# A fused gate, state-space and linear-attention kernel: the flag transpose becomes the last TensorE instruction, SP issues in emission order, and the hand-written order list is replaced

## The chip, the cores and the metric

The kernel runs on one core of a Trainium2 chip. The core has five engines with a queue of instructions each: TensorE (PE, matrix products), VectorE (DVE), ScalarE (ACT), GpSimd (POOL) and SyncE (SP, which computes nothing here and issues DMA transfers). They meet at semaphores. Each engine takes its instructions in the order of its own queue.

The metric is the device time of one execution in microseconds, here the median of nine.

## The reference

One input sequence x of 2048 rows and 512 columns goes through two branches, and a gate mixes them row by row.

```python
g = sigmoid((x * gate_w).sum(-1, keepdims=True))
# A: a diagonal complex state-space recurrence
Lam_bar = exp(dt * Lam);  Bu = einsum("bld,pd->blp", x, B_bar)
for t in range(L): h = Lam_bar * h + Bu[:, t];  hs.append(h)
a = 2 * einsum("blp,dp->bld", hs, Cmat).real + x * Dskip
# B: linear attention, 32 heads of 16
q, k, v = split(x @ wqkv)
phi_q = cat(softmax(q @ w_phi), softmax(-(q @ w_phi)));  phi_k likewise
kv = einsum("bhsf,bhsd->bhfd", phi_k, v);  z = phi_k.sum(s)
b = (phi_q @ kv / (phi_q @ z + 1e-6)) @ wo
return g * a + (1 - g) * b
```

## The kernel before

The 2048 rows are taken as 512 groups of four (`F = 4`), so row 4r + f belongs to phase f, and each phase is cut into four tiles of 128. The state space is handled in four scans (`scan_unit`, j = 0 to 3). For each, PE projects x with B (`g_unit`, line 676) and folds the phases (line 681), ACT or DVE copy the result out of PSUM into the tile `Gs` or, for the last phase, into a buffer `c` (lines 377 and 379). SP rearranges that buffer with four DMAs (`xd`, line 690, called the swap below), DVE rotates it and runs the recurrence (lines 714 to 732), and eight DMAs put the states into `Zs` (`zd`, line 744). `fill_unit` (lines 756 to 764) then derives the other three phases on DVE. The output matrix is scaled into an `ET` buffer (lines 599 and 604) and stored into `CT` with eight DMAs (`ctd`, line 611).

For the attention, `v_unit` (449) and `k_unit` (788, 812, 819) build the values, the key features and their sums; `q_unit` (876) and `smalls` build the query features and the scales. `mix` (line 972) then makes one output tile of 128 rows: four products with the key-value blocks (985), a copy by ACT (988) and scaling and adding by DVE (992, 994) into `o2`; a DMA transpose of `o2` to `oT` on SP (1009); the state-space product with `CT` (1001) and the skip term (1005) on PE; the product with `Wo` into the same PSUM (1017, function `pb`); the scaling by the gate on ACT or DVE (1022 or 1024, function `of`) and the output DMA (1028, `od`), on SP's or ACT's queue. The very last tile is made in two halves of 256 columns.

The fast path is valid only for inputs within limits. DVE collects them (`fl1`, 1047 to 1050), PE transposes the column of verdicts (1052), DVE reduces it to one integer (`fl2`, 1055 and 1056), and every engine loads that integer (`values_load`, 1062) and branches (line 162) past the code of a general path that stands behind.

What runs in which order is decided by a planner, `_Plan`. Every step is a task with an estimated cost for each engine that may run it, and the tuple `ORDER` gives the sequence in which tasks are placed and emitted; an entry is twice the task's number, plus one where the second engine listed takes it. The planner's times only choose buffers; `ORDER` fixes the sequence. `deps` and `follow` of a task enter those times, no semaphore comes from them. The set `ENGINES` (line 211) names the engines whose instructions stay in the order of emission. SP is not in it: its instructions are reordered by the language's own scheduler. Every engine's instructions wait at semaphores for the data and the buffers that they use. SP's queue does not pass over an instruction that waits.

Of the kernel before, what the change touches and what calls it, by code (L numbers as in the profile page):

```python
# [18 lines left out]
P = 128  # L19
# [103 lines left out]
def kernel(  # L123
# [58 lines left out]
    564, 422, 482, 400, 552, 484, 464, 466, 108, 486, 220, 222, 600, 554, 488, 110, 402, 566, 364, 410, 574, 556,  # L182
    412, 414, 224, 374, 216, 492, 468, 186, 626, 494, 112, 490, 594, 576, 416, 188, 496, 578, 558, 232, 376, 114,
    116, 218, 596, 234, 118, 580, 424, 604, 120, 498, 426, 598, 246, 602, 500, 428, 236, 692, 238, 606, 694, 584,
    226, 630, 248, 696, 430, 228, 122, 586, 632, 230, 628, 686, 588, 608, 640, 124, 642, 250, 718, 688, 458, 240,
    610, 724, 590, 560, 432, 126, 434, 252, 690, 592, 242, 722, 244, 612, 634, 726, 636, 644, 366, 652, 638, 370,
    128, 720, 728, 698, 582, 700, 654, 656, 198, 666, 372, 254, 646, 702, 616, 256, 668, 730, 368, 618, 648, 650,
    670, 704, 786, 200, 732, 436, 258, 734, 614, 278, 708, 658, 280, 660, 774, 710, 834, 620, 790, 792, 788, 662,
    736, 828, 672, 202, 816, 778, 712, 622, 838, 776, 836, 822, 740, 742, 796, 204, 624, 260, 664, 818, 714, 744,
    674, 716, 746, 780, 794, 748, 262, 826, 676, 832, 756, 752, 750, 824, 810, 130, 754, 820, 798, 784, 782, 812,  # L190
    814, 804, 1204, 846, 850, 852, 830, 802, 678, 738, 806, 848, 808, 854, 264, 1222, 840, 1216, 800, 856, 1210,
    948, 1226, 680, 858, 842, 862, 864, 950, 946, 844, 682, 866, 944, 868, 902, 1224, 1212, 1036, 870, 952, 860,
    976, 884, 1214, 954, 978, 996, 1002, 998, 878, 956, 984, 1076, 970, 1004, 1078, 980, 1080, 1048, 960, 972,
    958, 1074, 684, 1022, 974, 1050, 1062, 1006, 1000, 1024, 1054, 1056, 982, 1010, 1052, 1008, 1206, 872, 1028,
    962, 988, 1058, 964, 1060, 1218, 1038, 966, 1030, 968, 1014, 986, 1082, 1026, 1064, 874, 1084, 880, 1208,
# [6 lines left out]
    1198, 1282, 1148, 1177, 1350, 918, 1294, 1266, 1346, 1316, 1250, 1310, 1286, 1272, 1348, 1318, 1296, 920, 938,  # L202
    1284, 1252, 1288, 1200, 1290, 1364, 1366, 1352, 1416, 1292, 1358, 926, 1150, 1410, 1268, 922, 1270, 1324,
    1368, 1360, 1418, 932, 928, 1298, 1124, 1412, 1320, 1384, 1274, 924, 1420, 1202, 1414, 1390, 1322, 1362, 930,
    1276, 1422, 934, 1326, 936, 1386, 1278, 1370, 1300, 1428, 1436, 1372, 1328, 940, 942, 1424, 1392, 1442, 1376,
    1438, 1302, 1394, 1444, 1398, 1374, 1388, 1426, 1354, 1331, 1396, 1430, 1046, 1400, 1432, 706, 1440, 1446,
    1448, 1450, 1242, 1402, 1088, 772, 1305, 1435, 1378, 1357, 1380, 1468, 1404, 1454, 1452, 1407, 1409, 1456,
    1470, 1472, 1458, 1462, 1465, 1382, 1466, 1461)
KR = 0
GR = 0  # L210
ENGINES = {mybir.EngineType.PE, mybir.EngineType.DVE, mybir.EngineType.Activation, mybir.EngineType.Pool}


def _pe(n, cols):
    return {"PE": n * max(30.0, cols / 2.4 + 3.0)}


def _dve(*elems):
    return {"DVE": sum(e / 0.96 + 70.0 for e in elems)}


def _act(*elems):
    return {"ACT": sum(e / 1.2 + 100.0 for e in elems)}
# [3 lines left out]
def _fast_path(ctx, tc, A_x, A_Lambda_re, A_Lambda_im, A_B_re, A_B_im, A_C_re, A_C_im, A_log_dt, A_Dskip,  # L227
               B_wqkv, B_w_phi, B_wo, gate_w, out):
    nc = tc.nc
# [15 lines left out]
    def ctile(shape, dt, name):  # L245
        return const.tile(shape, dt, name=name)
# [9 lines left out]
    ident = ctile([P, P], BF16, "ident")  # L256
# [28 lines left out]
    fb = ctile([P, 2], BF16, "fb")  # L285
# [17 lines left out]

    ctx.enter_context(tc.manual_schedule(engines=ENGINES))

# [42 lines left out]
    pl = _Plan({"DVE": 2.4e3, "ACT": 5.6e3, "PE": 1.1e3, "SP": 27.0e3})  # L348
# [12 lines left out]
    def f32v(b):  # L361
        return b.t[:]

    def bfv(b):
        return b.t[:].bitcast(BF16)[:, 0:512]
# [18 lines left out]
    d_wv0, d_wv, d_b, d_wk, d_wq, d_wo = (pl.at(t) for t in (4.8, 5.6, 17.0, 22.7, 24.8, 27.0))  # L384
    d_vec, d_wc = pl.at(9.5), pl.at(20.5)

    def tcols(f, a):
        return slice(f * NCH + a * P, f * NCH + (a + 1) * P)
# [38 lines left out]
    for a in range(4):  # L427
# [5 lines left out]
        t = pl.add({"PE": 460.0} if a < 2 else _pe(4, 128), tr, deps=[d_x[a // 2]], follow=[t_warm], bufs=[b, early[0]])  # L433
# [145 lines left out]
    for jj in range(2):  # L579
        parts = []  # L580
        for tt in range(4 * jj, 4 * jj + 4):
# [3 lines left out]
                           deps=parts, rank=6 - jj))  # L585
# [10 lines left out]
    for j in range(PT):  # L596
        done = []
        for ri in range(2):
            done.append(pl.add(_act(640), lambda e, j=j, ri=ri: nc.scalar.mul(out=tC[:, ri, :], in_=cb.t[:, 1 - ri, j, :], mul=nb2i[:, j:j + 1]),
                               deps=[tp6, t_cl] + tc_b[-2:], bufs=[cb], rank=2))  # L600
# [15 lines left out]
    for jj in range(2):  # L616
# [10 lines left out]
        def tb3(e):  # L627
# [4 lines left out]
                    deps=[x2, t_trig], bufs=[early[2]], rank=5)  # L632
# [283 lines left out]
    def lb(k0, n, shape=None, dt=BF16):  # L916
        def make(k):
            if not late:
                late.append(wk.tile([P, NTI * H * (Dh + 1)], BF16, tag="vx", name="late", bufs=1))
            v = late[0][:, k0 + k * n:k0 + (k + 1) * n]  # L920
            v = v if dt is BF16 else v.bitcast(dt)
            return v if shape is None else v.rearrange("p (a b) -> p a b", a=shape)
        return make
# [2 lines left out]
    pl.pool("al", 2, lb(12 * D, 4 * 2 * H, 4))  # L926
    pl.pool("ot", 4, lb(13 * D, D))
    t_al, als, t_qm = {}, {}, []

    def smalls(f, rank=0.0):  # L930
        pl.unit("smalls")
# [40 lines left out]
    def mix(f, a, rank=0.0):  # L972
        pl.unit("mix")
        ti = f * 4 + a
        cs = slice(a * P, (a + 1) * P)
        last = (f, a) == (FO[3], 3)
        pys = [pl.buf(*A3) for _ in range(2 if last else 1)]
        w = D // len(pys)
        pn = [pl.buf(*A2), pl.buf(*A2)]
        o2 = pl.buf("o2")  # L980
        tm = []
        for sgn in range(2):
            def nm(e, sgn=sgn):
                for g in range(HG):
                    MM(out=f32v(pn[sgn])[:, g * P:(g + 1) * P], lhsT=ets[f].t[:, sgn, g, cs], rhs=KVbd[:, sgn, g, :], start=True, stop=True)  # L985
            t = pl.add(_pe(4, 128), nm, deps=t_kvx + [t_al[f]], bufs=[pn[sgn], ets[f], o2], rank=rank + 2)

            tn = pl.add(_act(512), lambda e, sgn=sgn: nc.scalar.copy(out=o2.t[:, sgn], in_=f32v(pn[sgn])), deps=[t], bufs=[pn[sgn], o2], rank=rank + 2)  # L988

            def sc(e, sgn=sgn):  # L990
                v = o2.t[:, sgn].rearrange("p (g d h) -> p g d h", g=HG, d=Dh)
                VT(out=v, in0=v, in1=als[f].t[:, a, sgn * H:(sgn + 1) * H].rearrange("p (g h) -> p g h", g=HG).unsqueeze(2).to_broadcast([P, HG, Dh, 8]), op=ALU.mult)  # L992
            tm.append(pl.add(_dve(256), sc, deps=[tn, t_al[f]], bufs=[o2, als[f]], rank=rank + 2))
        x = pl.add(_dve(256), lambda e: VT(out=o2.t[:, 0], in0=o2.t[:, 0], in1=o2.t[:, 1], op=ALU.add), deps=tm, bufs=[o2], rank=rank + 2)
        yh = []
        for hh in range(2):
            def ym(e, hh=hh):
                for tt in range(4 * hh, 4 * hh + 4):
                    st = Zs[:, 0, tt, ZP + a * P:ZP + (a + 1) * P] if f == 3 else Gs[:, tt, f, cs]
                    for n, py in enumerate(pys):  # L1000
                        MM(out=f32v(py)[:, 0:w], lhsT=st, rhs=CT[:, tt // 2 + 4 * (tt % 2), n * w:n * w + w], start=(tt == 0), stop=False)  # L1001
                if hh == 1:
                    for kt in range(KT):
                        c0 = kt * P % w
                        MM(out=f32v(pys[kt * P // w])[:, c0:c0 + P], lhsT=xT[:, kt, tcols(f, a)], rhs=Dd[:, kt, :], start=False, stop=False)
            c = _pe(4, 512)["PE"] + (hh * _pe(4, 128)["PE"])
            yh.append(pl.add({"PE": c}, ym, deps=[(t_z[j] if f == 3 else t_h[j, f]) for j in (2 * hh, 2 * hh + 1)] + [t_ct] + t_dd, follow=yh[-1:], bufs=pys, rank=rank))
        oT = pl.buf("oT")
        t = pl.add({"SP": 1200.0}, lambda e: nc.sync.dma_start_transpose(out=oT.t, in_=o2.t[:, 0]), deps=[x], bufs=[oT, o2], rank=rank + 3, xl={"SP": 700.0})

        ot = pl.buf("ot")
        for n, py in enumerate(pys):
            hs = slice(n * w, n * w + w)

            def pb(e, py=py, hs=hs):
                for g in range(HG):
                    MM(out=f32v(py)[:, 0:w], lhsT=oT.t[:, g, :], rhs=Wo[:, g, hs], start=False, stop=(g == HG - 1))  # L1017
            tb = pl.add(_pe(4, w), pb, deps=[t, d_wo], follow=yh[-1:], bufs=[py, oT], rank=rank + 3)

            def of(e, py=py, hs=hs):  # L1020
                if e == "ACT":
                    nc.scalar.mul(out=ot.t[:, hs], in_=f32v(py)[:, 0:w], mul=Gg[:, ti:ti + 1])  # L1022
                else:
                    VS(out=ot.t[:, hs], in0=f32v(py)[:, 0:w], scalar1=Gg[:, ti:ti + 1], scalar2=None, op0=ALU.mult)
            to = pl.add({"ACT": w / 1.2 + 200.0, "DVE": w / 0.96 + 135.0}, of, deps=[tb, t_gg], bufs=[py, ot], rank=rank + 3)

            def od(e, hs=hs):
                (nc.scalar if e == "ACT" else nc.sync).dma_start(out=o4[a, :, f, hs], in_=ot.t[:, hs])
            pl.add({"SP": 600.0, "ACT": 600.0}, od, deps=[to], bufs=[ot], rank=rank + 3, xl={"ACT": 1800.0 + 700.0 * (not last), "SP": 400.0 + 700.0 * (not last)})
# [14 lines left out]
    bf_ = pl.buf(*A2)  # L1044
# [4 lines left out]
        nc.vector.tensor_reduce(out=fl[:, 3:4], in_=fl[:, 0:3], axis=AX.X, op=ALU.max)  # L1049
        VS(out=fb[:, 0:1], in0=fl[:, 3:4], scalar1=GATE_LIMIT, scalar2=None, op0=ALU.is_le)  # L1050
    x = pl.add({"DVE": 600.0}, fl1, deps=t_qm + [t_fk, t_tn], rank=20)
    x = pl.add({"PE": 60.0}, lambda e: nc.tensor.transpose(bfv(bf_)[0:1, 0:P], fb[:, 0:1], ident[:]), deps=[x], bufs=[bf_], rank=20)

    def fl2(e):
        nc.vector.tensor_reduce(out=ff[:, 0:1], in_=bfv(bf_)[0:1, 0:P], axis=AX.X, op=ALU.min)
        VS(out=flag_i[:], in0=ff[:, 0:1], scalar1=-1.0, scalar2=1.0, op0=ALU.mult, op1=ALU.add)
    pl.add({"DVE": 400.0}, fl2, deps=[x], bufs=[bf_], rank=20, xl={"DVE": 2500.0})

    pl.run()
    tc.mark_branch_hint_location("general", engines=(mybir.EngineType.PE, mybir.EngineType.DVE, mybir.EngineType.Activation))  # L1060
# [622 lines left out]
```

## Time and profile before

| | |
|---|---|
| nine runs, median | 153.94 us |
| nine runs, lowest and highest | 153.58 and 155.66 us |
| profiled execution, its time | 154.16 us |
| profiled execution, its span | 152.4 us |
| ACT busy | 108.4 us (71%) |
| DMA moved | 14.96 MB, mean 98 GB/s |
| DMA transposes of `late` (line 1009), issue to landing, min / median / max | 2.4 / 2.5 / 3.9 us |

The span runs from the first to the last recorded instruction; the device time has some start and end around it. Rows give the start or the busy time in us, the line of the kernel, the engine, the operation and the tiles as output <- input; "SPq" and "ACTq" are an engine's queue, in which DMAs are issued. A number in brackets is idle time of that engine just ahead, and what ended it. Pool buffers taken late in the kernel are all called `late`, PSUM buffers `pp`.

### The profile page before, as it was taken

The numbers are of one execution on the slowest core, as the hardware profiler recorded it, in microseconds if no ns is written. First come the engines' busy times: TensorE is split into PE (matmuls) and PEld (weight loads), VectorE is DVE, ScalarE is ACT, GpSimd is POOL, SyncE is SP. The second block draws the span as 40 slices with busy tenths as digits, with TensorE's granted clock in tenths as the row PEclk, the third lists the DMA queues.
The fourth block names the chain that finished last, engine by engine and source line by source line (L and its number), as shares of the span: only waits on it lengthen the run. The fifth ranks groups of instructions, "written<-read, shape, count | busy, mean of one in ns | idle before, by whom it ended". The sixth has DMA issues, their size and how long they took to land.

```text
span 152.4 us, 3149 instructions
## 1 busy us (share of the span) xinstructions
PE 142.0 (93%) x1105; PEld 82.6 (54%) x1124; DVE 131.0 (86%) x373; ACT 108.4 (71%) x218; POOL 5.3 (3%) x16
## 2 busy tenths in 40 slices
PE   6699999999999999999999999999999999999930
PEld 1344667455656665465446556566556455555720
DVE  2349999899999999998999999899999999998120
ACT  3149978999789798987999999759754845373110
POOL 8500000000000000000000000000000000000000
PEclk9999999999999999999999999999999999999995
DMA  3999999900320333223530313232661185035430
GB/s 103 304 208 234 163 237 221 195 6 0 69 69 0 80 94 103 52 68 96 128 79 29 96 47 99 52 69 38 74 170 35 34 108 137 0 77 121 123 107 3
DMA packets 37260, 14.96 MB, mean 98 GB/s; under 512 B 29432, under 2 KB 37240, under 8 KB 37240
## 3 DMA queue, kind: packets, MB, share of 16 engines
q1 hardware_dynamic: 35488, 13.33, 40.7%
q10 hardware_dynamic: 1592, 1.38, 3.1%
q8 instruction: 10, 0.16, 0.5%
q14 instruction: 10, 0.08, 0.2%
q0 software_dynamic: 160, 0.01, 0.1%
HBM read 1.60 MB, written 2.10 MB: 24 GB/s over the span
## 4 chain that ended last, share of the span: by engine, by line
PE 41%; DVE 35%; DMA 9%; ACT 4%; SPq 4%; issue 2%; DVEq 0%; ACTq 0%
PE pp L1001 9%; PE pp L676 8%; PE pp L449 7%; PE pp L788 6%; PE pp L1017 5%; DMA Zs<-c 5%; DVE c L724 5%; DMA xn<-in_A_x_dram 3%; DVE c L760 3%; DVE E L812 3%; DVE late L992 3%; DVE st L805 2%; DVE ET L604 2%; SPq L744 2%; DVE c L757 2%
## 5 line engine op out<-in xcount | busy, mean ns | idle before, releaser
L676 PE MATMUL pp<-xT,BT 128*128 128x512 bf16 x122 | 30.6, 381 | 0.2
L1001 PE MATMUL pp<-CT,Gs 128*128 128x512 bf16 (+1 forms) x101 | 23.5, 362 | 0.4
L676 PEld LDWEIGHTS <-BT 128*128 128x128 bf16 x128 | 17.8, 145 | 8.5
L988 ACT CAST late<-pp 128x512 bf16<-128x512 f32 x32 | 17.8, 591 | 6.1 <-PE pp L985 5.0
L240 ACT ACTIVATE E<-pp 128x512 bf16<-128x512 f32 x32 | 17.4, 614 | 2.3 <-PE pp L819 1.7
L240 ACT ACTIVATE ET<-pp 128x512 bf16<-128x512 f32 x32 | 17.3, 602 | 0.4 <-PE pp L876 0.3
L1022 ACT ACTIVATE late<-pp,Gg 128x512 bf16<-128x512 f32 (+1 forms) x15 | 10.1, 679 | 10.0 <-PE pp L1017 7.1
L1017 PE MATMUL pp<-Wo,late 128*128 128x512 bf16 (+1 forms) x65 | 15.6, 366 | 0.2
L788 PE MATMUL pp<-Wk,xT 128*128 128x512 bf16 x64 | 15.8, 379 | 0.0
L449 PE MATMUL pp<-Wv,xT 128*128 128x512 bf16 x63 | 15.2, 379 | 0.3 <-DVE xT L379 0.3
L876 PE MATMUL pp<-xT,Wq 128*128 128x512 bf16 x61 | 14.5, 379 | 0.2
L1001 PEld LDWEIGHTS <-Gs 128*128 128x128 bf16 x104 | 9.5, 98 | 8.3 <-DVE Gs L764 1.1
L992 DVE TENSOR_TENSOR late<-late 128x512 bf16<-128x512 bf16 x32 | 12.8, 426 | 0.0
L377 ACT CAST Gs<-pp 128x512 bf16<-128x512 f32 x18 | 10.3, 598 | 3.4 <-PE pp L676 2.0
L985 PE MATMUL pp<-KVbd,ET 128*128 128x128 bf16 x128 | 11.3, 219 | 0.0
L985 PEld LDWEIGHTS <-ET 128*128 128x128 bf16 x128 | 8.7, 98 | 3.7
L377 ACT CAST vx<-pp 128x512 bf16<-128x512 f32 x16 | 8.9, 594 | 2.1 <-PE pp L449 2.1
L788 PEld LDWEIGHTS <-xT 128*128 128x128 bf16 x64 | 6.2, 98 | 7.2
L812 DVE TENSOR_TENSOR E<-E,rc 128x2048 bf16<-128x2048 bf16 x8 | 9.7, 1220 | 0.4 <-ACT rc L240 0.4
L876 PEld LDWEIGHTS <-Wq 128*128 128x128 bf16 x64 | 6.0, 98 | 6.6
L449 PEld LDWEIGHTS <-xT 128*128 128x128 bf16 x64 | 5.9, 98 | 6.8 <-DVE xT L379 0.5
L724 DVE TENSOR_TENSOR_SCAN c<-sp,c 128x512 bf16<-128x512 f32 x8 | 9.3, 1210 | 0.0
(171 smaller groups left out, 242.6 us busy)
## 6 DMA issues: line engine op xcount, KB each, us to landing
Zs<-c SPq DMA_DIRECT2D x32, 64.0 KB, 2.1
c<-c SPq DMA_DIRECT2D x16, 64.0 KB, 2.0
CT<-ET SPq DMA_DIRECT2D x8, 128.0 KB, 3.0
out_dram<-late ACTq DMA_DIRECT2D x8, 128.0 KB, 1.9
out_dram<-late SPq DMA_DIRECT2D x7, 128.0 KB, 1.9
xn<-in_A_x_dram SPq DMA_DIRECT2D x2, 256.0 KB, 4.3
Wo<-in_B_wo_dram SPq DMA_DIRECT2D x4, 128.0 KB, 3.1
Wv<-in_B_wqkv_dram ACTq DMA_DIRECT2D x1, 256.0 KB, 4.2
```

The lines of the kernel that those rows point to most:

```text
L240: return nc.scalar.activation(**kw)
L377: nc.scalar.copy(out=o, in_=view(b))
L449: MM(out=f32v(b), lhsT=xT[:, kt, tcols(f, a)], rhs=Wv[:, kt, :], start=(kt == 0), stop=(kt == KT - 1))
L676: MM(out=f32v(b), lhsT=BT[:, kt].rearrange("p r (q t) -> p (r q) t", t=NT)[:, :, j + 4 * h], rhs=xT[:, kt, f * NCH:(f + 1) * NCH], start=( ...
L724: nc.vector.tensor_tensor_scan(out=bw_.t[:, ri], data0=rb, data1=b1.t[:, ri], initial=0.0, op0=ALU.mult, op1=ALU.add)
L788: MM(out=f32v(b), lhsT=xT[:, kt, tcols(f, a)], rhs=Wk2[:, kt, :], start=(kt == 0), stop=(kt == KT - 1))
L876: MM(out=f32v(b), lhsT=Wq2[:, kt, g * P:(g + 1) * P], rhs=xT[:, kt, f * NCH:(f + 1) * NCH], start=(kt == 0), stop=(kt == KT - 1))
L985: MM(out=f32v(pn[sgn])[:, g * P:(g + 1) * P], lhsT=ets[f].t[:, sgn, g, cs], rhs=KVbd[:, sgn, g, :], start=True, stop=True)
L988: tn = pl.add(_act(512), lambda e, sgn=sgn: nc.scalar.copy(out=o2.t[:, sgn], in_=f32v(pn[sgn])), deps=[t], bufs=[pn[sgn], o2], rank=rank + 2)
L992: VT(out=v, in0=v, in1=als[f].t[:, a, sgn * H:(sgn + 1) * H].rearrange("p (g h) -> p g h", g=HG).unsqueeze(2).to_broadcast([P, HG, Dh, 8]) ...
L1001: MM(out=f32v(py)[:, 0:w], lhsT=st, rhs=CT[:, tt // 2 + 4 * (tt % 2), n * w:n * w + w], start=(tt == 0), stop=False)
L1017: MM(out=f32v(py)[:, 0:w], lhsT=oT.t[:, g, :], rhs=Wo[:, g, hs], start=False, stop=(g == HG - 1))
```

## The change

The task of the flag's transpose gets a `follow` on the last `pb`, the estimate of the flag's way is changed, SP joins the set of engines that keep emission order, and `ORDER` is a new list. As written, the list moves few tasks: the flag's transpose and reduction stand behind the last product with `Wo` (the tail `1470, 1472` moves behind `1462`), the scaling of the second half of the last tile goes from DVE to ACT (`1465` becomes `1464`), one ACT copy of `Gs` (`628`) comes ahead of an ACT scaling and a small activation, one DVE reduction into `smax` (`706`) comes six instructions earlier, and a task of ACT (`844`) and one of SP (`1428`) move against tasks of other engines. On PE nothing else moves.

Because SP now follows the list, its queue changes more. The four swaps of scan 1 stand together, the first of them waiting for the later of two tiles; scan 2's four swaps stand ahead of scan 1's stores to `Zs`; the eight stores to `CT`, spread over the scans before, stand together behind the swaps of scan 3. Behind the `Zs` stores came, in order, with T a transpose and O an output: TTTTO TTTO TO TTO TO TTO TTTO, the flag's load, O. Now it is TTTTTTTO TTTO TTOOO TTO TTO O, the flag's load, with the sixth and seventh T in the other order.

```diff
-    226, 630, 248, 696, 430, 228, 122, 586, 632, 230, 628, 686, 588, 608, 640, 124, 642, 250, 718, 688, 458, 240,
+    226, 630, 248, 696, 430, 228, 628, 122, 586, 632, 230, 686, 588, 608, 640, 124, 642, 250, 718, 688, 458, 240,
...
-    948, 1226, 680, 858, 842, 862, 864, 950, 946, 844, 682, 866, 944, 868, 902, 1224, 1212, 1036, 870, 952, 860,
+    948, 1226, 680, 858, 842, 862, 864, 950, 946, 682, 866, 944, 868, 844, 902, 1224, 1212, 1036, 870, 952, 860,
...
-    1276, 1422, 934, 1326, 936, 1386, 1278, 1370, 1300, 1428, 1436, 1372, 1328, 940, 942, 1424, 1392, 1442, 1376,
-    1438, 1302, 1394, 1444, 1398, 1374, 1388, 1426, 1354, 1331, 1396, 1430, 1046, 1400, 1432, 706, 1440, 1446,
+    1276, 1422, 934, 1326, 936, 1386, 1278, 1370, 1300, 1436, 1372, 1328, 706, 940, 942, 1424, 1428, 1392, 1442,
+    1376, 1438, 1302, 1394, 1444, 1398, 1374, 1388, 1426, 1354, 1331, 1396, 1430, 1046, 1400, 1432, 1440, 1446,
     1448, 1450, 1242, 1402, 1088, 772, 1305, 1435, 1378, 1357, 1380, 1468, 1404, 1454, 1452, 1407, 1409, 1456,
-    1470, 1472, 1458, 1462, 1465, 1382, 1466, 1461)
+    1458, 1462, 1470, 1472, 1464, 1382, 1466, 1461)
...
-ENGINES = {mybir.EngineType.PE, mybir.EngineType.DVE, mybir.EngineType.Activation, mybir.EngineType.Pool}
+ENGINES = {mybir.EngineType.PE, mybir.EngineType.DVE, mybir.EngineType.Activation, mybir.EngineType.Pool, mybir.EngineType.SP}
...
+    t_pb = None
...
+        nonlocal t_pb
...
-            tb = pl.add(_pe(4, w), pb, deps=[t, d_wo], follow=yh[-1:], bufs=[py, oT], rank=rank + 3)
+            tb = t_pb = pl.add(_pe(4, w), pb, deps=[t, d_wo], follow=yh[-1:], bufs=[py, oT], rank=rank + 3)
...
-    x = pl.add({"PE": 60.0}, lambda e: nc.tensor.transpose(bfv(bf_)[0:1, 0:P], fb[:, 0:1], ident[:]), deps=[x], bufs=[bf_], rank=20)
+    x = pl.add({"PE": 60.0}, lambda e: nc.tensor.transpose(bfv(bf_)[0:1, 0:P], fb[:, 0:1], ident[:]), deps=[x], follow=[t_pb], bufs=[bf_], rank=20)
...
-    pl.add({"DVE": 400.0}, fl2, deps=[x], bufs=[bf_], rank=20, xl={"DVE": 2500.0})
+    pl.add({"DVE": 400.0}, fl2, deps=[x], bufs=[bf_], rank=20, xl={"DVE": 2300.0})
```

## The prediction

> **What bounds the kernel now.** I read the page first: busy shares, then slices.
>
> ```profile
> PE 142.0 (93%) x1105; PEld 82.6 (54%) x1124; DVE 131.0 (86%) x373; ACT 108.4 (71%) x218; POOL 5.3 (3%) x16
> PE   6699999999999999999999999999999999999930
> ```
>
> TensorE (PE) is full from the third slice to the 38th; then come about 6 us without a matmul. The view of stretches says how full, with PE busy in the third column:
>
> ```profile
> 10.00:140.00 130.00, 128.40 (x1024) 75.56 (x1042) 125.25 (x344) 104.05 (x212) 0.00 (x0) 1.00 0.43 92
> 140.00:146.20 6.20, 6.15 (x47) 3.87 (x44) 1.71 (x7) 1.85 (x3) 0.00 (x0) 1.00 0.45 130
> 146.20:152.40 6.20, 0.00 (x0) 0.00 (x0) 0.48 (x1) 0.00 (x0) 0.00 (x0) 0.67 0.14 29
> ```
>
> PE idles 1.60 us of 130: nothing done for DVE, ACT or SP in the middle can gain more, and whatever stalls PE costs in full. The last 6.2 us are a tail in which no engine computes. The timeline from 140 us shows its start (start, length, engine, line):
>
> ```profile
> 144.86 0.60 PE L1017 MATMUL pp<-Wo,late 128*128 128x256 bf16 x4
> 145.39 0.22 PE L1052 MATMUL pp<-ident,fb 128*1 128x128 bf16 x1
> 145.50 0.47 ACT L1022 ACTIVATE late<-pp,Gg 128x256 bf16<-128x256 f32 x1 [1.71 <-PE pp L1017]
> 145.54 0.61 PE L1017 MATMUL pp<-Wo,late 128*128 128x256 bf16 x4
> 145.65 0.28 DVE L1055 TENSOR_REDUCE ff<-pp 1x1 f32<-1x128 bf16 x1 [0.93 <-PE pp L1052]
> 146.25 0.48 DVE L1024 TENSOR_SCALAR late<-pp,Gg 128x256 bf16<-128x256 f32 x1
> 147.05 0.34 SPq L1028 DMA_DIRECT2D out_dram<-late  x1
> ```
>
> The flag's transpose stands between the two halves of the last output tile; the second half's DMA leaves 0.31 us after its data (147.05 against 146.25 + 0.48). The views of lines 1062 and 162 say why, and what follows:
>
> ```profile
> L1062 SPq TENSOR_LOAD <-flag_i x1: 482/482/482, 146.1 to 146.1; - x1
> L1062 SPq FUSED_REGOPS  x1: 192/192/192, 146.7 to 146.7; - x1
> L162 SPq EVENT_SEMAPHORE  x8: 17/17/17, 148.0 to 150.7; - x8
> L162 SPq COMPARE_BRANCH  x1: 58/58/58, 147.4 to 147.4; - x1
> ```
>
> SP reads the flag (146.13), then issues the last DMA, branches, and waits for eight DMA semaphores until 150.75. In its records five waits pass at 147.98 to 148.31 in steps of 0.085, and the sixth, for this DMA, at 150.61. From the eighth (150.75) to the span's end lie 1.61 us, a fixed chain of semaphores and drains. The DMA views, of the last 7 us and of the whole:
>
> ```profile
> q14 instruction: 4, 0.03, 1.9%
> q8 instruction: 1, 0.02, 1.0%
> out_dram<-late SPq DMA_DIRECT2D x1, 64.0 KB, 3.5
> ```
>
> ```profile
> out_dram<-late SPq DMA_DIRECT2D x7, 128.0 KB, 1.9
> ```
>
> Half the bytes took 3.5 us where full tiles take 1.9. The packet records show five instruction fetches of 8 to 16 KB at 147.78 to 148.98, each 1.1 to 1.4 us after an engine's branch (146.70 to 147.44). Of the DMA's 16 completions 12 came by 148.65, four at 149.99 to 150.60. An earlier output, beside a fetch at 142.44, is spread the same way (143.16 to 145.17). So the tail is the last output colliding with the code that the branches fetch.
>
> **The change, part by part.**
>
> *1. Flag transpose after the last matmuls.* In the records the first half's fourth matmul starts at 145.19 and the second half's first at 145.54; two such matmuls without a transpose between lie 0.109 apart, so that start becomes 145.30 and all is 0.25 earlier: the last matmul ends at 145.90, not 146.16. The flag follows it: its weight load came 0.20 after the matmul ahead, its result at 0.42. Put behind the matmul of 145.63 it is ready at 146.05 (145.61 before), and the two DVE steps, unchanged, give the flag at 146.55 (146.10 before): 0.44 later. The planner's changed 2300 for 2500 is in its estimate only, 0.
>
> *2. Second half scaled on ACT instead of DVE.* ACT starts 0.04 after PE (145.466 to 145.503 for the first half): 145.94 + 0.475 = 146.42. DVE ended at 146.73. The first half's DMA on ACT's queue was issued at 146.01 and now stands behind the wait for the second half, which ends at 145.94: still 146.01. Nothing else waits behind it but ACT's flag load, before 146.39, now 146.57. DVE is left with the flag.
>
> *3. SP in emission order, tail.* The last DMA goes out at 146.44 (0.03 after ACT, as the DMA at 143.82 did), not 147.05: -0.6. Then SP loads the flag: 146.44 + 0.34 + 0.05 = 146.83, branch at 147.70 (load to assertion took 0.83). POOL, PE and DVE load at 146.57 and branch at about 147.15, so fetches start at 148.2. The DMA's packets began 0.84 after issue and ended 1.19 after: 147.3 to 147.6, ahead of all fetches. It lands, at 1.9, by 148.34. SP's first wait stands 0.54 after its branch, 148.24, the sixth 0.43 later at 148.67: the data is there. Eighth 148.84, + 1.61 = 150.45. Against 152.36: **-1.91**.
>
> *4. SP in emission order, middle.* 97 DMAs in a fixed order; I compared the readiness of each with its new place. (a) Scan 1's swap (L690): two of four issued at 48.48, now all wait for the tile ready at 52.04; the last goes at 53.9, lands at 2.0: 55.9; DVE wants it at 56.91. Slack 1.0. (b) Scan 2's swap was stuck behind a Zs store waiting for DVE (two rows of SP's timeline, one of DVE's):
>
> ```profile
> 65.92 0.48 SPq L744 DMA_DIRECT2D Zs<-c  x1
> 66.49 1.19 SPq L690 DMA_DIRECT2D c<-c  x2
> 69.21 0.69 DVE L714 TENSOR_TENSOR c<-c,Tcs 128x1024 bf16<-128x1024 bf16 x1 [0.98 <-DMA c<-c]
> ```
>
> Its data was ready at 64.79; it now goes first, lands by 67.5, and the 0.98 us of DVE vanish. PE did not idle for it: 0 to -0.3. (c) All eight CT stores (L611) move behind scan 3's swap: 76.3 to 81.3, landing (3.0) by 84.3; PE's first use is at 90.71, ACT's reuse of the ET buffer at 87.72, the Zs store behind is ready at 81.50. Cost 0. (d) Outputs against transposes: the sixth and seventh transposes (L1009) swap; the one issued at 110.19 goes at 112.4, lands (2.5) at 114.9; PE wants it at 115.68: slack 0.8, the thinnest. Four outputs go later, the worst (112.75) at 136.7, landing 138.6; ACT's reuse of its buffer is at 140.28. The other transposes go within 0.3 of now. POOL issues its loads as before.
>
> *5. ACT copy of Gs ahead of tC and rc; smax reduction earlier on DVE.* The copy's data was done at 53.6; it takes 0.48 where ACT idled 0.45 (60.22 to 60.67); rc is then ready at 60.7, DVE wants it at 61.76. The reduction of 0.28 moves within DVE's stream, which has slack there against PE. 0.
>
> **A rule against it.** The trace: each engine resumes 0.48 to 0.61 us after its branch, before its fetch shows a packet (SP: branch 147.44, next record 147.98, packet 148.52, done 148.98). The Trainium skill, "Runtime: NRT & Kernel Launch", section "Instruction fetch mechanics", says that a taken branch to code outside the loaded window has to fetch it by DMA before execution goes on. By the row SP pays 0.54; by the rule it stands until 147.70 + 1.54 = 149.24, 1.0 more: 151.45, a gain of 0.9. I take the row; the code behind the branch is the same.
>
> **Sum.** The profiled execution took 154.16 with a span of 152.36; the median of nine is 153.94. 152.36 - 1.91 = 150.45, + 1.80 around the span = 152.25; on the median, 0.22 lower: **152.0**.
>
> **The rivals.**
> *A (chance 0.70): as summed*, 151.3 to 152.7; the low end has 0.3 of PE idle recovered and 0.4 for a shorter landing or barrier, the high end 0.7 for waits that come out longer than their rows.
> *B (0.20): the tail gives little.* If fetches collide less in ordinary executions than in the profiled one, completion at 148.65 already ends the old kernel at 150.4, and the gain is nil; if SP pays the fetch, 0.9. For: four late packets decide it. Against: the nine times lie as near 154.16 as the profile. 152.7 to 154.0, middle 153.3.
> *C (0.06): slower, the swapped transpose stalls PE.* At 115.68 PE has no other work ready in its order. The stall is 112.4 + landing - 115.68; it starts at a landing of 3.3, and beats the 1.9 of the tail from 5.2 on. The longest landing seen is 3.9 (stall 0.6); at 7 us, 3.7: 153.94 - 1.91 + 3.7 = 155.7. Against: 2.4 to 2.5 is usual, and the long ones stand near a fetch.
> *D (0.04): it doesn't do what it says*: the last DMA still meets a fetch; 1.9 stays, only parts 1 and 2 count, 0.6: 153.3.
>
> **How the numbers follow.** A measurement tells about 1% from no change; that is 1.54 us, so faster means under 152.40. A lies under it with 0.85 (0.60 in all). Same takes the rest of A (0.10) and B and D but for 0.01 (0.23). Slower is C and that 0.01, 0.07. The range takes in A and most of B: 151.2 to 153.8.
>
> **What would show it.** Last matmuls evenly spaced and ending 0.25 earlier; scaling of both halves on ACT; last output issued before SP's flag load and landing in about 1.9, its completions not spread; SP's eight waits at one spacing; span near 150.5; DVE's wait of 0.98 at L714 gone. Wrong: a gap in PE before L1017 near 115, or SP's waits standing still after the branch.

## The result and the profile after

The changed kernel takes 151.88 us (median of ten, 151.45 to 153.3) against 153.94 in the same comparison (31 runs): a ratio of 0.986, 95% interval 0.983 to 0.989. The prediction said 152.0, with a range of 151.2 to 153.8. The profiled execution took 152.21 us with a span of 150.3; the one before had 154.16 and 152.4.

In some executions TensorE stays longer at the slow rate at which it starts, and the last matmul then ends up to 1.9 us later, with no change to the kernel; the ratios leave out executions more than 1.5% above the fastest of their kernel. So profiles are compared here by their *tail*, from the end of the last 256-column matmul to the end of the span: 152.36 - 146.16 = 6.20 us before, 150.31 - 145.79 = 4.52 after.

The page of the changed kernel, busy shares and TensorE's slices:

```profile
PE 142.8 (95%) x1105; PEld 83.2 (55%) x1124; DVE 130.7 (87%) x372; ACT 108.8 (72%) x219; POOL 5.3 (4%) x16
...
PE   6999999999999999999999999899999999999980
```

The last but one slice is now busy to eight tenths, where it was three. The view of stretches (PE busy in the third column; the third column from the right is the granted TensorE clock):

```profile
10.00:140.00 130.00, 128.50 (x1025) 75.57 (x1043) 125.32 (x345) 104.03 (x212) 0.00 (x0) 1.00 0.48 92
140.00:145.90 5.90, 5.90 (x46) 3.92 (x44) 1.21 (x4) 1.89 (x4) 0.00 (x0) 1.00 0.47 135
145.90:150.40 4.50, 0.03 (x1) 0.00 (x0) 0.42 (x2) 0.39 (x1) 0.00 (x0) 1.00 0.15 41
```

PE is busy 128.50 of the 130 us in the middle (128.40 before): SP's new order there changed it by 0.1 at most. The granted clock is 1.00 up to the last matmul in both kernels, so it has no part in the difference. PE ends 0.37 earlier, and the tail behind it is 1.68 shorter; together these are the 2.05 us of the span. The timeline of the end:

```profile
144.75 1.04 PE L1019 MATMUL pp<-Wo,late 128*128 128x256 bf16 x8
145.38 0.91 ACT L1024 ACTIVATE late<-pp,Gg 128x256 bf16<-128x256 f32 x2 [1.71 <-PE pp L1019]
...
145.71 0.22 PE L1054 MATMUL pp<-ident,fb 128*1 128x128 bf16 x1
145.89 0.34 ACTq L1030 DMA_DIRECT2D out_dram<-late  x1
145.97 0.28 DVE L1057 TENSOR_REDUCE ff<-pp 1x1 f32<-1x128 bf16 x1 [1.36 <-PE pp L1054]
146.28 0.14 DVE L1058 TENSOR_SCALAR flag_i<-ff 1x1 int32<-1x1 f32 x1
```

Eight matmuls in one row of 1.04 us: the hole that the transpose made is closed. Both halves are scaled on ACT, and the flag follows. SP's own timeline, then what SP does at the flag's load and at the branch:

```profile
146.32 0.33 SPq L1030 DMA_DIRECT2D out_dram<-late  x1
```

```profile
L1064 SPq TENSOR_LOAD <-flag_i x1: 527/527/527, 146.7 to 146.7; - x1
L1064 SPq FUSED_REGOPS  x1: 192/192/192, 147.3 to 147.3; - x1
L1064 SPq SEQ_ASSERT  x1: 37/37/37, 147.5 to 147.5; - x1
```

```profile
L162 SPq EVENT_SEMAPHORE  x8: 17/17/17, 148.2 to 148.7; - x8
...
L162 SPq COMPARE_BRANCH  x1: 58/58/58, 147.6 to 147.6; - x1
```

The output goes first, the load second. The eight waits pass within 0.54 us, where before the sixth alone stood for 2.3. The DMA view of the last 6 us:

```profile
q14 instruction: 4, 0.03, 1.7%
q8 instruction: 1, 0.02, 1.1%
...
out_dram<-late SPq DMA_DIRECT2D x1, 64.0 KB, 1.6
```

The same five instruction fetches are still there. The output of the same size lands in 1.6 us in place of 3.5. In the records behind this view its 16 completions come at 147.78 to 147.94, before the first fetch at 148.14; before, they came at 148.47 to 150.60, with fetches from 147.78 on.

### The profile page after: what moved, and what is told of

Its sections match the earlier page's. It is cut to its first block, busy times and chain, and to the rows that moved or that the text cites. A ratio compares the mean times of both kernels' runs of the same rounds, so it can differ in the third digit from the quotient of the medians.

```text
span 150.3 us, 3144 instructions
## 1 busy us (share of the span) xinstructions
PE 142.8 (95%) x1105; PEld 83.2 (55%) x1124; DVE 130.7 (87%) x372; ACT 108.8 (72%) x219; POOL 5.3 (4%) x16
## 4 chain that ended last, share of the span: by engine, by line
PE 63%; DVE 17%; DMA 8%; ACT 3%; SPq 2%; issue 2%; DVEq 0%; ACTq 0%
PE pp L676 18%; PE pp L1002 9%; PE pp L788 9%; PE pp L449 9%; DMA Zs<-c 6%; PE pp L1019 5%; PE pp L681 4%; DVE c L760 3%; DVE late L993 3%; SPq L744 2%; DMA xn<-in_A_x_dram 2%; DVE c L757 2%; PE pp L819 2%; PE pp L876 2%; DVE Gs L764 2%
## 5 line engine op out<-in xcount | busy, mean ns | idle before, releaser
L449 PE MATMUL pp<-Wv,xT 128*128 128x512 bf16 x63 | 15.7, 387 | 0.1
```

The costliest lines, as they stand in the source:

```text
L449: MM(out=f32v(b), lhsT=xT[:, kt, tcols(f, a)], rhs=Wv[:, kt, :], start=(kt == 0), stop=(kt == KT - 1))
```

## The experiments

In every table and text below, *distance* is the time from the issue of the last output on its queue to the first packet of an instruction fetch behind the branches, and *spread* the time from the first to the last of that output's 16 completions. Both are read from the DMA records of one profiled execution, as the tail is. The ratio is that of the times to the kernel before, on the same chip; the medians are of all runs.

| kernel | median us (runs) | ratio, 95% interval | distance | spread | tail |
|---|---|---|---|---|---|
| before | 153.94 (31) | 1 | 0.73 | 2.13 | 6.20 |
| changed | 151.88 (10) | 0.986 (0.983 to 0.989) | 1.82 | 0.16 | 4.52 |
| 1a before, no branch | 151.9 (4) | 0.989 (0.983 to 0.996) | no fetch | 0.13 | 3.57 |
| 1b changed, no branch | 150.81 (4) | 0.980 (0.975 to 0.986) | no fetch | 0.14 | 3.31 |
| 2a before, SP keeps emission order | 153.44 (22) | 0.996 (0.993 to 0.999) | 1.02 | 1.00 | 4.83 |
| 2b changed, SP free | 152.29 (13) | 0.991 (0.987 to 0.994) | 1.80 | 0.16 | 4.53 |
| 2c before, flag last | 151.83 (7) | 0.990 (0.986 to 0.993) | 2.00 | 0.13 | 4.60 |
| 2d changed, flag between | 152.21 (22) | 0.992 (0.989 to 0.995) | 1.28 | 0.26 | 4.52 |
| 2e changed, half on DVE | 151.96 (7) | 0.992 (0.987 to 0.997) | 1.99 | 0.15 | 4.60 |
| 3 changed, output late | 155.0 (15) | 1.010 (1.007 to 1.013) | below 0 | 0.13 | 7.75 |
| 4a changed, no assertion | 152.68 (6) | 0.993 (0.990 to 0.996) | 1.81 | 0.16 | 4.19 |
| 4b the same again | 151.28 (8) | 0.983 (0.979 to 0.987) | 1.80 | 0.15 | 4.19 |
| 4c also output from ACT | 151.36 (6) | 0.986 (0.981 to 0.991) | 1.81 | 0.16 | 3.98 |
| changed again, beside 3, 4b, 4c | 151.5 (6) | 0.985 (0.980 to 0.990) | 1.80 | 0.16 | 4.53 |

**1. Take the branch away, from both kernels.** The general path and the branch to it are left out; the flag is computed and loaded as before.

```diff
-    with tc.If(flag_i != 0, label="general"):
-        general_path(tc, A_x, A_Lambda_re, A_Lambda_im, A_B_re, A_B_im, A_C_re, A_C_im, A_log_dt, A_Dskip,
-                     B_x, B_wqkv, B_w_phi, B_wo, gate_w, out)
...
-    tc.mark_branch_hint_location("general", engines=(mybir.EngineType.PE, mybir.EngineType.DVE, mybir.EngineType.Activation))
```

> The kernel before, without the branch and the general path behind it (the flag is still computed and loaded). Theory 'fetch': the last output lands late in the kernel before because the code that the branches fetch collides with it. Here nothing is fetched at the end: the output, issued near 147.05, lands in 1.6 to 1.9 us with its completions close together; span 149.7 to 150.6, time 151.5 to 152.3. Rival 'order': the gain of the changed kernel comes from SP's order in the middle; then only the branch itself (about 0.5) goes: span 151.7 to 151.9, landing still 3.5. Rival 'two queues': the late completions come from the two output DMAs of the last tile meeting each other: landing still 3.5.

> The changed kernel, without the branch and the general path. Theory 'fetch': its last output was already clear of the fetch (1.6), so only the branch's own 0.53 and some of the eight waits go: span 149.1 to 149.9, and the distance between this pair of kernels is 0.3 to 0.9 where it is 2.1 with the branch. Rival 'order': the distance of 2.1 stays.

The DMA view of the end of the kernel before without its branch has no instruction queue any more, and the output is as quick as in the changed kernel:

```profile
q10 hardware_dynamic: 288, 0.20, 8.9%
q1 hardware_dynamic: 144, 0.07, 3.3%
...
out_dram<-late SPq DMA_DIRECT2D x1, 64.0 KB, 1.6
```

SP still loads the flag first there and issues the output second, with DVE's half ahead of it. So neither SP's order nor DVE's half makes 3.5 us out of 1.6; the branch and the fetches that come with it do. With the branch the tails of the two kernels are 1.68 apart, without it 3.57 - 3.31 = 0.26. About 1.4 us of the 1.68 go with the branch. The span of 1a is 149.2, a little below the range that I had expected. The medians of this pair are 1.1 apart, above the 0.3 to 0.9 expected, and rest on four runs each, with intervals that overlap a little; the profiles carry this reading, and experiment 3 shows the fetches at work packet by packet.

**2. One part of the change alone, or one part undone.** First SP's place in the set: added to the kernel before (2a), taken out of the changed one (2b, where SP's scheduler puts its middle back as it was before, and still issues the last output ahead of the load).

```diff
-ENGINES = {mybir.EngineType.PE, mybir.EngineType.DVE, mybir.EngineType.Activation, mybir.EngineType.Pool}
+ENGINES = {mybir.EngineType.PE, mybir.EngineType.DVE, mybir.EngineType.Activation, mybir.EngineType.Pool, mybir.EngineType.SP}
```

> The kernel before, with SP alone added to the set that keeps emission order. SP's middle is that of the changed kernel; the last output goes at 146.76 instead of 147.05, ahead of SP's flag load, but the other four engines still branch at 146.7 to 146.9. Theory 'fetch': their fetches from 147.8 still meet its packets (147.6 to 147.95), at least the late ones: completions partly spread, span 150.9 to 152.1, time 152.5 to 153.7. Rival 'order': the whole gain, span 150.3, time 151.9.

> The changed kernel, but SP out of the set that keeps emission order: SP's middle is then that of the kernel before, while the last output still stands ahead of SP's flag load. Theory 'fetch': as the changed kernel, span 150.1 to 150.6, time 151.7 to 152.2; DVE's wait of about 1.0 at L714 is back and costs nothing, PE having no idle for it. Rival 'order': the gain is lost, time 153.5 to 154.

The DMA view of 2a's end shows a value between the two:

```profile
out_dram<-late SPq DMA_DIRECT2D x1, 64.0 KB, 2.5
```

15 completions came at 147.54 to 147.78, one at 148.54, with fetches from 147.11 on. Its 22 times lie anywhere from 151.8 to 154.7, and the profiled execution (152.2) is among the quick ones: the number of completions caught may differ from one execution to the next, which a single profile cannot show. 2b has the changed kernel's tail to 0.01 us, so SP's place in the set is not needed for the tail. DVE's wait ahead of L714 is back in it (1.00 us), as expected. In time 2b gained 0.9%, the changed kernel 1.4%, and the intervals overlap a little: that SP's order in the middle is worth some tenths of a us is neither shown nor excluded.

Then the flag's place alone, moved in the kernel before (2c):

```diff
-    1470, 1472, 1458, 1462, 1465, 1382, 1466, 1461)
+    1458, 1462, 1465, 1470, 1472, 1382, 1466, 1461)
```

> The kernel before with only the end of the order list changed, so that the flag transpose and its two small operations stand behind the last matmuls; the second half stays on VectorE, SP's order in the middle of the kernel stays as before. Theory (the last output must not be on its way while the branches fetch their code): the four other engines' branches move about 1.3 us later and their fetches to about 148.5, the last output lands before them without spread, the end comes 4.5 to 4.9 us after the last matmul (6.2 before, 4.53 in the changed kernel) and the time is 151.9 to 152.4, nearly the whole gain of the change. Rival (SP's own place in the order, or the half on ScalarE, carries the gain): output still spread over 2 us and 153.4 to 153.9.

Its timeline shows what this one line does:

```profile
144.40 1.04 PE L1017 MATMUL pp<-Wo,late 128*128 128x256 bf16 x8
...
145.54 0.48 DVE L1024 TENSOR_SCALAR late<-pp,Gg 128x256 bf16<-128x256 f32 x1 [1.28 <-ACT late L1022]
...
145.94 0.27 DVE L1055 TENSOR_REDUCE ff<-pp 1x1 f32<-1x128 bf16 x1
146.05 0.33 SPq L1028 DMA_DIRECT2D out_dram<-late  x1
146.24 0.14 DVE L1056 TENSOR_SCALAR flag_i<-ff 1x1 int32<-1x1 f32 x1
```

The flag is written at 146.38, 0.33 after the output's issue started. SP issues the output ahead of its load of the flag (146.43), and all branches come after it. 151.83 us: this one line gives 1.0% (0.7 to 1.4), the whole change 1.4% (1.1 to 1.7): the greater part of the gain, and within the intervals perhaps all of it.

The reverse, the flag's place undone in the changed kernel (2d), and the half given back to DVE (2e):

```diff
-    1458, 1462, 1470, 1472, 1464, 1382, 1466, 1461)
+    1470, 1472, 1458, 1462, 1464, 1382, 1466, 1461)
...
-    x = pl.add({"PE": 60.0}, lambda e: nc.tensor.transpose(bfv(bf_)[0:1, 0:P], fb[:, 0:1], ident[:]), deps=[x], follow=[t_pb], bufs=[bf_], rank=20)
+    x = pl.add({"PE": 60.0}, lambda e: nc.tensor.transpose(bfv(bf_)[0:1, 0:P], fb[:, 0:1], ident[:]), deps=[x], bufs=[bf_], rank=20)
```

> The changed kernel with the flag transpose and its two small operations put back ahead of the last matmuls; SP's new order and the half on ScalarE stay. Theory of the fetches: the last output is issued as early as in the changed kernel but the other engines branch earlier, their fetches (about 147.7) meet its packets (147.4 to 147.9), some of these are held, and the end comes 4.8 to 6.0 us after the last matmul: 152.3 to 153.7. Rival (SP's order and the half on ScalarE carry it): 4.5 us and the time of the changed kernel, 151.7 to 152.1.

```diff
-    1458, 1462, 1470, 1472, 1464, 1382, 1466, 1461)
+    1458, 1462, 1465, 1470, 1472, 1382, 1466, 1461)
```

> The changed kernel with the second half's scaling on VectorE as before, the flag still last. Theory of the fetches: the half on ScalarE is worth nothing or up to 0.3 us, the output lands unspread, the end comes 4.5 to 4.9 us after the last matmul, 151.8 to 152.3. Rival (the half on ScalarE is part of the gain): 152.6 or more.

2e came as the theory had it. For 2d I had expected a tail of 4.8 to 6.0, and the profile showed 4.52: three fetches do start at 147.75 to 147.78, ahead of the output's completions (147.97 to 148.23), yet only one completion is late, by 0.12 against the one before it. So "no fetch before the landing" is too strict. In these rows the spread falls as the distance grows: 0.73, 1.02, 1.28 and 1.8 to 2.0 us go with 2.13, 1.00, 0.26 and 0.13 to 0.16. The packet records give the reason. A packet is one of the pieces in which a DMA moves its data. Wherever no fetch comes between, the packets of SP's last output run from 0.83 to 1.19 us after its issue, and the completions follow some 0.4 later. At 1.28 all packets are through (147.65) before the first fetch (147.75); at 1.02 the first fetch starts among them. And no single part of the change is indispensable for the tail: flag last alone, or SP's order with the half on ACT, each bring the distance above 1.19.

**3. Make the distance small again in the changed kernel.** Three DMAs of 128 bytes go ahead of the last output on SP's queue.

```diff
+    spare = ctile([1, 3, 64], BF16, "spare")
...
-            def od(e, hs=hs):
+            def od(e, hs=hs, n=n):
+                for k in range(3 if last and n == 1 else 0):
+                    nc.sync.dma_start(out=spare[0:1, k, :], in_=ot.t[0:1, hs.start:hs.start + 64])
```

> The changed kernel with three small DMAs (128 bytes each, from the scaled half to a spare word of SBUF) issued by SP ahead of the last output, which is thereby issued about 1.0 us later; the flag is still last and the other engines branch as in the changed kernel. The runs so far stand in a row by the distance from the issue of the last output to the first fetch behind the branches: 0.73 us in the kernel before (completions up to 2 us late), 1.02 in the one with only SP in the barrier list (one completion 0.8 late), 1.28 with the flag between (one 0.1 late), 1.82 in the changed kernel (none). Theory of that distance: here it is about 0.8, so the last completions are late by 1 to 2 us, and the end comes 6.0 to 7.2 us after the last matmul, 153.3 to 154.5. Rival (the early flag itself, not the distance, spreads the output): SP's chain is later by 1.0 and nothing else, 5.5 us after the last matmul, 152.9, completions within 0.2 of each other.

SP's timeline at the end, and the DMA view:

```profile
146.17 1.88 SPq L1032 DMA_DIRECT2D spare<-late  x3
148.11 1.59 SPq L1033 DMA_DIRECT2D out_dram<-late  x1
```

```profile
q14 instruction: 3, 0.02, 1.2%
q8 instruction: 1, 0.02, 1.0%
...
out_dram<-late SPq DMA_DIRECT2D x1, 64.0 KB, 2.8
```

Neither expectation held, and the tail of 7.75 lies above both: the small DMAs took SP 0.6 each, not 0.33, and the output, meant for a distance of 0.8, was issued 0.1 *after* the first fetch began (148.01). It was not spread (150.82 to 150.95); instead its issue took 1.59 in place of 0.33. The small DMAs in front of it tell the rest, in one execution, with three fetches recorded at 148.01, 148.16 and 148.19. The first, 1.83 us ahead of them, has a spread of 0.16. The second, 1.17 ahead, has 13 completions by 148.56 and three at 149.50, 149.74 and 150.38. The third, 0.54 ahead, has 13 by 149.18 and three at 149.67, 149.92 and 150.55. So distance alone does not decide: 1.17 spreads this DMA by 2 us, more than 1.02 spreads the output of 2a.

The packets do. Those of the first small DMA end at 147.58, ahead of all fetches. Of the second's, 13 of the 16 that close it start at 148.07 to 148.22, while the fetches begin. The other three start at 148.46, 148.63 and 149.34, and at just these times, to 0.01 us, the three fetches end. So each fetch holds some of the packets until it is done. That it holds those of the DMA engine which carries it is the likeliest reading; which engine carried what is not in the records. The completions of the held packets come another 1.04 to 1.11 us later, against some 0.3 for the others; why is open. In the third DMA the three late completions follow those of the second by 0.17 each.

The same reading fits the other kernels. In 2a one fetch (147.11) starts before the output's packets are through (147.27); the packets that it holds go on at 147.54, where it ends, and one completion is late. In the kernel before, three fetches start before the packets would have been through (148.24); held packets go on at 148.37, 148.79 and 149.05, where these three end. Four completions are late; for the fourth, a fetch that starts at 148.37 comes into question. In 2d and the changed kernel no fetch starts in time, and no packet is held. The records of experiment 3 have four fetches in all, the others five, so one may be missing.

**4. Shorten what now sets the end.** In the changed kernel SP's own chain is last: load 146.71, register work and assertion until the branch at 147.63, waits from 148.16, eighth at 148.70, end 1.61 later. Take the assertion out (4a, 4b); then let ACT issue the output that it has scaled, so that SP has only the flag (4c).

```diff
-    return nc.values_load(flag_i[0:1, 0:1], min_val=0, max_val=1)
+    return nc.values_load(flag_i[0:1, 0:1], min_val=0, max_val=1, skip_runtime_bounds_check_because="one minus a comparison")
...
-    1458, 1462, 1470, 1472, 1464, 1382, 1466, 1461)
+    1458, 1462, 1470, 1472, 1464, 1382, 1461, 1467)
```

> The changed kernel without the bounds assertion on the value that the engines load for the branch. SP's register instructions between its load and its branch go away, about 0.3 us. If SP's own chain (output issue, load, register work, branch, waits) sets the end, as the trace of the changed kernel suggests, the end comes about 4.2 us after the last matmul in place of 4.53 and the time is about 151.5. If the other engines' earlier branches (also about 0.3 us) bring their fetches onto the output's packets, the output is spread again and nothing or less is gained: 152 to 153.

> The changed kernel without the bounds assertion, once more, now beside the changed kernel on the same chip: its end came 4.19 us after the last matmul, yet its median of six was 152.68. If that median was chance (two kinds of executions some 1 us apart), it is 0.3 us below the changed kernel here; if the shorter tail is given back, the same or above.

> The changed kernel without the bounds assertion and with the last output issued by ScalarE, which scales that half, so that SP has nothing to issue and loads the flag as soon as it is written. If SP's own chain sets the end, SP branches about 0.25 us earlier than without the assertion alone, and the end comes 3.9 to 4.1 us after the last matmul (4.53 in the changed kernel, 4.19 without the assertion), 151.2 to 151.5. If the landing of the last output or another engine's end holds it: 4.2 or more.

> The changed kernel itself, as the yardstick of this set: 151.9, 4.5 us from the last matmul to the end.

The tail shortened as worked out: 4.19 both times, and 3.98 with the output on ACT. In 4a SP branches 0.07 after its load's end (146.94 + 0.52 = 147.46), where the changed kernel needs 0.39 (147.24 to 147.63). Its rows at the branch:

```profile
L162 SPq EVENT_SEMAPHORE  x8: 17/17/17, 148.1 to 148.6; - x8
...
L162 SPq COMPARE_BRANCH  x1: 58/58/58, 147.5 to 147.5; - x1
```

Branch and waits stand 0.1 earlier than in the changed kernel although the last matmul ended 0.23 later (146.02). In time the gain is not resolved. I had expected about 151.5 for 4a. The first set gave 152.68 (six runs, 151.70 to 152.96), the second 151.28 beside 151.5 for the changed kernel, whose intervals overlap. 4c took 151.36, no less than 4b. The lowest times of the second set are 151.07 for 4b, 151.19 for 4c and 151.37 for the changed kernel: a gain of 0.2 to 0.3 is possible, and these runs don't prove it.

## Why the prediction came out right, point by point

*What bounds it.* That the tail was the last output's collision with the fetched code is what experiments 1 and 3 show. That the middle had little to give fits PE's busy time (128.50 against 128.40) and the tail of 2b; a gain of some tenths there is not excluded.

*1, flag last.* PE's end was foretold at 145.90 and came at 145.79, the last second-half matmuls at an even 0.109; the extra 0.11, which was not foretold, is a start 0.115 earlier (143.65 against 143.77 for the last product with `CT`). Most of it comes from a hole ahead of 109.84, 0.15 before and 0.05 now; what closed it is open. The flag came at 146.42 (146.55 foretold), 0.13 earlier with PE.

*2, half on ACT.* It ended at 146.29, against 146.42. Experiment 2e says what it was worth by itself: a tail 0.08 longer without it, and nothing that shows in time.

*3, SP in the tail.* Output issued 146.32 (146.44), SP's branch 147.63 (147.70), waits 148.16 to 148.70 (148.24 to 148.84), end 150.31 (150.45). From PE's end the tail was foretold at 4.55 and came at 4.52, so the right number is no luck of errors that cancel. The condition was right too: the packets were to be ahead of all fetches, and they were through at 147.51, the first fetch at 148.14. Only the landing was mis-sized: 1.6, where I took the 1.9 of full tiles, and the sixth wait was not waiting for it anyway. What the prediction got wrong here is the credit. The 1.91 is the sum of parts 1 to 3 but stands under SP's emission order. The runs show that this order is one of several ways to the same end: with the flag last it is not needed for the tail (2b, 2c), and without that (2a) it gives 0.4% of the time.

*4, SP in the middle.* DVE's wait of 0.98 ahead of the swap's consumer did vanish: the timeline of DVE has no bracket there any more. But further on it has a new one:

```profile
68.17 0.69 DVE L714 TENSOR_TENSOR c<-c,Tcs 128x1024 bf16<-128x1024 bf16 x1
...
82.51 0.43 DVE L858 TENSOR_TENSOR KVbd<-pp,mask 64x256 bf16<-64x256 f32 x1 [0.86 <-PE pp L819]
```

DVE runs ahead and then waits 0.86 for PE, which sets the pace: of the gain of "0 to -0.3" nothing shows. The landing of the `CT` stores was mis-sized: median 5.3 and longest 6.1, not 3.0. The last was issued at 81.0, so all were there by 87.1 at the latest, still ahead of ACT's reuse of the buffer (87.75) and of PE's first use (90.76). The thinnest slack, the transpose issued at 112.4, held: PE has no bracket between 106 and 118. Rival C is out.

*5.* PE's busy time from 10 to 140 us changed by 0.1; 0 fits.

*The rule weighed.* The row was right. SP's first wait stands 0.53 after its branch (147.63, 148.16), while the last fetch shows its packet at 148.83. The Trainium skill, "Runtime: NRT & Kernel Launch", section "Instruction fetch mechanics", has a taken branch wait for its fetch when the target is outside the loaded window; by that SP would have stood until after 149.1 and the span would have ended about 1 us later. Whether SP's next instructions lay outside the window no record shows, so the page is neither confirmed nor refuted. What a fetch cost here, it cost a transfer on its way.

*Rival B* needed ordinary executions to collide less than the profiled one. Its forecast was 153.3; the ratio excludes that. *Rival D*, the output still meets a fetch, didn't happen. In 2a, with 0.8 us less distance, it does in part.

## What to carry to other kernels

When a kernel ends in a branch or otherwise jumps to code that is fetched, get the packets of the last output through before the first fetch starts. Here they were through 1.19 us after the issue (1.4 for a 128-byte copy within SBUF); an output that fetches caught finished 2 us late. Look at the packets, not at the completions. Moving the branch's condition *later* can make a kernel faster if it keeps the fetches behind the last transfer. When a change has several parts, run each alone: here one line of the order list gave most or all of what the whole was credited with.

## What the runs showed of the hardware that was not expected

An instruction fetch holds some packets of a data DMA until it ends: in experiment 3 the three held packets that close a DMA start at the ends of three fetches, to 0.01 us, and their completions come 1.04 to 1.11 us later still, where 0.3 is usual.

The issue itself can be held. SP's issues took 1.59 us for the output of experiment 3, and in the changed kernel 1.76 for the output at 124.27 and 1.51 for the store to `Zs` at 69.11. Each started within 0.3 us of a 16 KB fetch (148.19, 124.02 and 69.04). SP's other outputs in the changed kernel took 0.33 to 0.58. It is no rule for every fetch: a store at 91.92, 0.3 after an 8 KB fetch, took 0.6 like its neighbours, and an output that ACT issued at 108.91, 0.17 after a 16 KB fetch, took 0.39.

The 128-byte DMAs took SP 0.6 us each to issue, as much as the 64 KB swaps, which also go from SBUF to SBUF (0.59 in the median): the size made no difference.

TensorE starts at about 0.63 us for a 128x512 matmul and goes over to 0.38, and the moment varies from execution to execution. In the `v_unit` products of the kernel before the slowest took 390 ns:

```profile
L449 PE MATMUL pp<-Wv,xT x63: 377/379/390, 5.6 to 77.9; 128*128 128x512 bf16 x63
```

In the profile of the changed kernel that was run again the same line reads

```profile
L449 PE MATMUL pp<-Wv,xT x63: 376/379/634, 5.6 to 79.7; 128*128 128x512 bf16 x63
```

In the first the last matmul at the full slow rate starts at 4.65, in the second at 9.96, and in the other profile of the changed kernel at 6.88. The record of the granted clock begins at the same moment: at 4.92, 10.63 and 7.07. Between the two profiles of the changed kernel the first product behind the slow stretch (L484) already differs by 1.86 (10.26 and 12.12), and so does the end of the last matmul (145.79 and 147.65). What decides the moment is open.
